# Gate weights in three blocks per half instead of two, and the parameter rows moved from SyncE's load queue to GpSimd's

## The chip, the core and the metric

The kernel runs on one core of a Trainium2 chip. The metric is the device time of one execution in microseconds (us). The core has five engines with a queue each: TensorE (PE, with its weight loads as PEld), VectorE (DVE), ScalarE (ACT), GpSimd (POOL) and SyncE (SP). SP and ACT also issue loads and stores, which 16 DMA engines carry out; in the profile q1 is SP's DMA queue and q10 is ACT's. Each engine runs its instructions in the order of the program and waits on semaphores for the others.

## The reference

What is computed, for one sequence of 2048 tokens with 448 channels:

```python
xn = _layernorm(x)
# A: a diagonal complex state space, 448 states
dt = exp(log_dt); Lam_bar = exp(dt * Lam)
B_bar = ((Lam_bar - 1) / Lam)[:, None] * Bmat
h = Lam_bar[None, :] * h + Bu[:, t, :]          # for every token t
s = 2 * einsum("blp,dp->bld", hseq, Cmat).real + xn * Dskip
# B: a gated unit, 448 -> 1792 -> 448
g = xn @ w_gate; u = xn @ w_up
b = (sigmoid(g) * u) @ w_down
out = x + s * silu(b)
```

## The kernel before

**Tiles and stages.** The tokens are 16 tiles of 128 (x tile t), in four chunks of 512. Each tile is normalised, transposed to channels by tokens (xnT), and multiplied with the gate and up weights: 14 steps a chunk, seven for `g` and seven for `u`. A step makes 256 of the 1792 features of one matrix, 128 with the weights and inputs in partitions 0 to 63 (L688) and 128 with those in 64 to 127 (L689): the 448 channels are seven groups of 64, and each weight matrix lies in one tile, wG or wU, with half of its columns in each half of the partitions. A step writes one of three PSUM buffers (gu). ScalarE takes a `g` step out with a tanh (L702), VectorE a `u` step with the product (L705); only then can the buffer be written again. Between the steps TensorE makes the input of the state space (`b_units`, L736 to L752), which ScalarE copies to bus (L760) and VectorE turns, scans and turns back (`ssm_pair`, L796 to L820; `ssm_stack`, L830 and on), the down projection (L864) and the output of the state space (L889).

**The first chunk** is different. Its gate and up weights are still being loaded. Its four x tiles come in three loads (tile 0 by SP, 1, and 2 with 3, by ACT). `stats` takes mean and variance on VectorE (L421, L422); `chain` takes the root on ScalarE (L430), copies the mean on GpSimd (`meanf`, L431) and inverts the root on VectorE (L432); `norm` (L449) makes xn. TensorE transposes (`pe_transpose`, L481 to L483), and ScalarE (tile 0, L486) or VectorE (L489) copies the result to xnT. `warm_mm` fills TensorE until then. The first three `g` steps are split in halves of tokens: with tiles 0 and 1 as soon as these are there, with tiles 2 and 3 later.

**The loads at the head.** A half of the gate matrix (1792 columns in two halves, 64 partitions each) comes in blocks of steps, which `BLK` lists. Half 0 is loaded by SP, half 1 by ACT, so a block needs a load of each. The three parameter vectors (log_dt, Lambda_im, Lambda_re) are loaded by `load_p` as three rows of one partition each into vrow, a piece of an hF tile. `columns` turns them with five small matmuls (L521, L523) and a copy (L527) into columns pv. GpSimd makes from them, in six small operations from L535 to L544, the step dt, the angle `turn` and the radius `r`. `tables` needs `turn`: ScalarE scales an index row (L556), VectorE reduces the angle (L558, L560), ScalarE takes Abs, Sin and Cos (L563 to L567). `coeffs` (GpSimd) and `c_scale` follow.

After the gate weights SP issues the up weights (two blocks of each half), x tiles 4 to 7, and `dbc`, then the transposed loads of B (L373 by `tload`). x tiles 4 to 7 are the input of chunk 1: `stats` (L421), `chain` on GpSimd (L435, L436) with a reciprocal and a product on VectorE (L438, L439), `norm` on ScalarE (L454), and a skip row on VectorE (L462, `skip_row`).

**What sets the order.** Every operation is handed to a planner (`Plan`), with an engine, an assumed cost, and the keys that it reads (`r`) and writes (`w`). `solve` gives each a due time, backward from a fixed order of TensorE's operations, then plays the program forward with the assumed costs: a free engine takes, of what is ready, what is due first. The instructions are emitted in the order of these planned starts, and each engine then keeps that order. TensorE's order is that of the calls, and VectorE's too while `pl.seq` is set (at the head). So an assumed cost, a rate or a moved call can change the order on the other engines.

**Load slots.** Loads and stores of SP and ACT share eight completion semaphores, taken in turn. The ninth load waits, on its issuing engine and with all that is queued behind it, until the first has landed, and so on. In the program before, SP's second gate block is the ninth and waits for x tile 0, ACT's second gate block is the tenth and waits for the first parameter row, and the first up load, the eleventh, waits for the first gate block. The planner imitates this:

```python
k = o.slot if o.slot < HEAD_DMA else max(HEAD_DMA, len(landed))
if k - 8 in landed:
    o.end = free[e] = max(o.end, landed[k - 8] + o.cost)
```

Loads that GpSimd issues have semaphores of their own and are planned with 6 us from issue to landing.

Of the kernel before, what the change touches and what calls it, by code (L numbers as in the profile page):

```python
# [14 lines left out]
ACT = mybir.ActivationFunctionType  # L15
# [3 lines left out]
D = 448  # L19
# [54 lines left out]
class Plan:  # L74
# [10 lines left out]
    def add(self, eng, cost, fn, r=(), w=(), dma=0, lat=None, chain=False, name="", rate=230e3):  # L85
        o = Op()
        o.idx, o.eng, o.cost, o.fn, o.dma, o.name = len(self.ops), eng, cost, fn, dma, name
        o.lat = LAT.get(eng, 0.0) if lat is None else lat
        o.pre, o.suc, o.rate = {}, [], rate
        o.slot = None  # L90
        if dma and eng != "POOL":
            o.slot, self.n_dma = self.n_dma, self.n_dma + 1
        o.start = o.end = None
        for k in r:
            if k in self.w:
                self._edge(self.w[k], o, True)
        for k in w:
            for q in self.r.get(k, ()):
                self._edge(q, o, False)
            if k in self.w:  # L100
                self._edge(self.w[k], o, True)
        for k in w:
            self.w[k] = o
            self.r[k] = []
        for k in r:
            if k not in w:
                self.r.setdefault(k, []).append(o)
        if chain or eng == "PE" or (eng == "DVE" and self.seq):
            key = ("chain", eng)
            if key in self.last_of:  # L110
                self._edge(self.last_of[key], o, None)
            self.last_of[key] = o
        self.ops.append(o)
        return o
# [131 lines left out]
def kernel(  # L246
# [24 lines left out]
    def sbt(name, shape, dt=BF16):  # L271
        return sb.tile([P] + list(shape), dt, name=name)

    def flat(t, *dims):
        if len(dims) == 1:
            return t
        names = "abcd"[:len(dims)]
        kw = {n: v for n, v in zip(names[1:], dims[1:])}
        return t.rearrange("p (" + " ".join(names) + ") -> p " + " ".join(names), **kw)
# [41 lines left out]
    vrow = hF_raw[0][0:3, 0:448]  # L321
# [10 lines left out]
    def C(name, n=4, dt=FP32):  # L332
        if name not in col:
            col[name] = sbt("c_" + name, [n], dt)
        return col[name]
# [13 lines left out]
    def load(eng, key, nbytes, o, i, cost=0.45, r=(), rate=230e3):  # L349
        e = {"SP": Q, "ACT": A, "POOL": G}[eng]  # L350
        add(eng, cost, lambda: e.dma_start(out=o, in_=i), w=[key] if not isinstance(key, list) else key,  # L351
            r=r, dma=nbytes, chain=True, rate=rate)

    def load_x(t0, n, q="SP", r=(), rate=230e3):
        load(q, [("x", t) for t in range(t0, t0 + n)], n * P * D * 2,
             x_all[:, t0:t0 + n, :], x_src[:, t0:t0 + n, :], r=r, rate=rate)

    BLK = {"g": [(0, 3), (3, 7)], "u": [(0, 3), (3, 7)]}

    def load_w(eng, k, half, b, r=(), rate=105e3):  # L360
        m0, m1 = BLK[k][b]
        ps = slice(half * H, half * H + H)
        c0 = half * 896
        load(eng, [("w", k, half, m) for m in range(m0, m1)], H * 7 * (m1 - m0) * P * 2,
             wgt[k][ps, :, m0 * P:m1 * P],
             wsrc[k][:, c0 + m0 * P:c0 + m1 * P].rearrange("(s p) f -> p s f", p=H), cost=0.65, r=r, rate=rate)
# [22 lines left out]
        add(e, 0.7, lambda: None, chain=True)  # L389
    add("ACT", 0.05, lambda: A.preload_act_table_set("sqrt_and_others"), w=["sqrttab"], lat=1.5, chain=True)  # L390

    def load_p(eng, k):
        load(eng, ("vrow", k), D * 2, vrow[k:k + 1, :], (A_log_dt, A_Lambda_im, A_Lambda_re)[k].unsqueeze(0), cost=0.25)
    load_x(0, 1, "SP")
    load_p("SP", 0)
    load_w("SP", "g", 0, 0)
    load_x(1, 1, "ACT")
    load_x(2, 2, "ACT")
    load_w("ACT", "g", 1, 0)
    load_p("SP", 1)  # L400
    load_p("SP", 2)
    load_w("ACT", "g", 1, 1)
    load_w("SP", "g", 0, 1)
    for h in range(2):
        load_w("SP", "u", h, 0, rate=215e3)
    load_x(4, 4, rate=300e3)
# [60 lines left out]
    def next_acc():  # L467
        a = acc_n[0] % 2
        acc_n[0] += 1
        return a  # L470
# [4 lines left out]
    def pe_transpose(t):  # L475
        b, a, js = t % NXN, next_acc(), slice(t * P, t * P + P)
        tp = flat(acc[a][:].bitcast(BF16)[:, 0:7 * P], 7, P)

        def f():
            for s in range(6):  # L480
                T.transpose(tp[:, s, :], xn[b][:, s * H:s * H + P], ident[:, :])  # L481
            T.transpose(tp[0:H, 6, :], xn[b][:, 384:448], ident[:, :])
            T.transpose(tp[H:P, 6, :], xn[b][:, 0:H], ident[:, :])  # L483
        add("PE", 0.46, f, r=[("xn", b), "ident"], w=[("acc", a)])
        if t == 0:
            add("ACT", 0.85, lambda: A.copy(out=xnT[0][:, :, js], in_=tp[:, :, :]),  # L486
                r=[("acc", a)], w=[("xnT", 0, t, "a"), ("xnT", 0, t, "b")])
        else:
            add("DVE", 0.64, lambda: V.tensor_copy(out=xnT[0][:, :, js], in_=tp[:, :, :]),  # L489
                r=[("acc", a)], w=[("xnT", 0, t, "a"), ("xnT", 0, t, "b")])  # L490
# [9 lines left out]
    def xr(c, lo=0, hi=TPC):  # L500
        return [("xnT", c % 3, j, h) for j in range(lo, hi) for h in "ab"]
# [13 lines left out]
    def columns():  # L515
        a = next_acc()
        vps = flat(acc[a][:, 0:12], 4, 3)

        def f():
            for i in range(3):  # L520
                T.matmul(vps[:, i, :], lhsT=vrow[:, i * P:(i + 1) * P], rhs=ident[0:3, 0:3], start=True, stop=True)  # L521
            for h in range(2):
                T.matmul(vps[h * H:h * H + H, 3, :], lhsT=vrow[:, 384:448], rhs=ident[0:3, 0:3], start=True, stop=True)  # L523
        add("PE", 0.4, f, r=["ident"] + [("vrow", k) for k in range(3)], w=[("acc", a)])
        pv = sbt("pv", [3, 4], FP32)
        dt_b = C("dt", 4, BF16)
        add("DVE", 0.1, lambda: V.tensor_copy(out=pv[:].rearrange("p k i -> p i k"), in_=vps[:]), r=[("acc", a)], w=["pv"])  # L527
        dt_b = C("dt", 4, BF16)
        lim, lre = pv[:, 1, :], pv[:, 2, :]
        K.update(lre=lre, lim=lim)  # L530
        eb = expc[:].to_broadcast((P, 4))

        def small(fn, r, w):
            add("POOL", 0.4, fn, r=r, w=w)
        tt = lambda o, x, y, op: (lambda: G.tensor_tensor(out=o, in0=x, in1=y, op=op))  # L535
        theta, arg, turn, r_col = C("theta"), C("arg"), C("turn"), C("r")
        small(tt(dt_b[:], eb, pv[:, 0, :], ALU.pow), ["pv", "expc"], ["dt"])
        small(tt(theta[:], dt_b[:], lim, ALU.mult), ["dt", "pv"], ["theta"])
        small(lambda: G.tensor_single_scalar(out=turn[:], in_=theta[:], scalar=1.0 / TWO_PI, op=ALU.mult),
             ["theta"], ["turn"])  # L540
        small(lambda: G.tensor_single_scalar(out=turn[H:P, 3:4], in_=theta[H:P, 3:4], scalar=-1.0 / TWO_PI,
                                            op=ALU.mult), ["theta", "turn"], ["turn"])
        small(tt(arg[:], dt_b[:], lre, ALU.mult), ["dt", "pv"], ["arg"])
        small(tt(r_col[:], eb, arg[:], ALU.pow), ["arg", "expc"], ["r"])  # L544
# [135 lines left out]
    def gu_mm(c, k, m, a, lo, hi, first):  # L680
        x = xnT[c % 3]
        ts = slice(lo * P, hi * P)
        w_ = wgt[k]
        ms = slice(m * P, m * P + P)

        def f():
            for s in range(7):
                T.matmul(gu[a][:, 0, ts], lhsT=w_[0:H, s, ms], rhs=x[0:H, s, ts], start=(s == 0), stop=(s == 6))  # L688
                T.matmul(gu[a][:, 1, ts], lhsT=w_[H:P, (s + 1) % 7, ms], rhs=x[H:P, s, ts],  # L689
                         start=(s == 0), stop=(s == 6))  # L690
        n = (hi - lo) * P
        return add("PE", 7 * (0.0028 + n / 2400.0) + (2 * SW if first else 0), f,
                   r=xr(c, lo, hi) + [("w", k, 0, m), ("w", k, 1, m)], w=[("gu", a)], name=f"{k}{c}.{m}")
# [234 lines left out]
    warm_mm(2)  # L928
    gu_mm(0, "g", 0, slots0[0], 0, 2, True)
    gu_mm(0, "g", 1, slots0[1], 0, 2, True)  # L930
    columns()
    pe_transpose(2)
    pe_transpose(3)
    silu_table()
    pl.seq = False
    gu_mm(0, "g", 2, slots0[2], 0, 2, True)
    for m in range(3):
        gu_mm(0, "g", m, slots0[m], 2, 4, False)
        gu_evac(0, "g", m, slots0[m])
# [143 lines left out]
```

## Time and profile before

| | us |
|---|---|
| median of 5 runs (lowest, highest) | 189.85 (188.67, 190.17) |
| the profiled execution | 190.17 |
| its span, first to last instruction | 188.3 |
| TensorE busy in the span | 180.3 |
| VectorE busy in the span | 168.6 |
| end of the warm-up matmuls, first gate matmul | 7.23, 8.94 |
| x tiles 4 to 7: issued, first used | 10.23, 17.80 |
| first L556 (tables) | 13.20 |

The page gives, for each engine, the time in which it was busy, its share of the span and the number of instructions, and then the span in 40 slices of 4.7 us, each with a digit for the busy share in tenths. Lines of waits give who waited, for whom, and how long in total, how often, and at longest. Lines of a timeline give start, duration, engine, line, operation, the tiles written and read, and, in brackets, the idle time before and what ended it. A load's issue and its landing are two things: the issuing queue shows the first, the landing follows some microseconds later.

### The profile page before, as it was taken

What the parts mean: (1) busy time and instruction counts of PE and PEld (TensorE: products, weight loads), DVE (VectorE), ACT (ScalarE), POOL (GpSimd) and SP (SyncE); (2) the same over time, 40 slices, a digit from 0 to 9 for tenths busy, and PEclk for the clock granted to TensorE, in tenths of its full rate; (3) what the DMA queues carried; (4) which work ended last, traced back from release to release, by engine and by line L of the source; (5) the groups of instructions that cost most, each with busy time, mean ns of one, the idle gap of its engine ahead of it and who ended that gap; (6) DMA issues with size and microseconds to landing.
All of it is one profiled execution on the core that took longest, in us unless ns stands there. A gap on an engine that the chain in (4) does not pass through costs nothing.

```text
span 188.3 us, 3507 instructions
## 1 busy us (share of the span) xinstructions
PE 180.3 (96%) x1375; PEld 89.2 (47%) x1375; DVE 168.6 (90%) x303; ACT 87.7 (47%) x124; POOL 32.5 (17%) x84
## 2 busy tenths in 40 slices
PE   7699999999999999999999999999999999999990
PEld 2286554474454444444454445444445445455560
DVE  3836799998999999989999998999999999899943
ACT  3529998735879651244547331337246221502110
POOL 3145447000014560000027800000000000000000
PEclk9999999999999999999999999999999999999999
DMA  6999999499400033200000343000000100000220
GB/s 164 234 208 249 163 135 222 98 248 146 172 3 0 0 77 73 49 0 3 0 2 0 77 101 70 0 28 0 24 3 0 49 0 28 0 24 28 73 77 24
DMA packets 29239, 13.43 MB, mean 71 GB/s; under 512 B 19619, under 2 KB 29222, under 8 KB 29222
## 3 DMA queue, kind: packets, MB, share of 16 engines
q1 hardware_dynamic: 27878, 12.05, 30.7%
q10 hardware_dynamic: 1344, 1.15, 2.6%
q8 instruction: 11, 0.18, 0.4%
q14 instruction: 6, 0.05, 0.1%
HBM read 6.77 MB, written 1.84 MB: 46 GB/s over the span
## 4 chain that ended last, share of the span: by engine, by line
PE 74%; DVE 10%; DMA 6%; SPq 6%; issue 1%; ACT 1%; DVEq 0%
PE gu L688 31%; PE acc L864 17%; PE acc L889 11%; PE gu L749 7%; PE gu L864 6%; DVE hF L705 5%; DMA wG<-in_B_w_gate_dram 4%; SPq L373 3%; SPq L351 3%; DMA bT<-in_A_B_re_dram 2%; DVE xd L462 1%; PE gu L752 1%; PE gu L736 1%; PE gu L889 1%; DVE z L799 1%
## 5 line engine op out<-in xcount | busy, mean ns | idle before, releaser
L688 PE MATMUL gu<-xnT,wG 64*128 64x512 bf16 (+1 forms) x224 | 46.5, 350 | 1.7 <-DMA wG<-in_B_w_gate_dram 1.7
L689 PE MATMUL gu<-xnT,wG 64*128 64x512 bf16 (+1 forms) x224 | 46.4, 350 | 0.0
L688 PE MATMUL gu<-xnT,wU 64*128 64x512 bf16 (+1 forms) x203 | 46.2, 369 | 0.2 <-ACT sig L702 0.2
L689 PE MATMUL gu<-xnT,wU 64*128 64x512 bf16 (+1 forms) x203 | 46.2, 369 | 0.0
L702 ACT ACTIVATE sig<-gu 128x1024 f32<-128x1024 f32 x21 | 21.4, 1022 | 33.3 <-PE gu L689 33.3
L864 PE MATMUL acc<-wd,hF 128*128 128x448 bf16 x168 | 33.8, 353 | 0.0
L864 PEld LDWEIGHTS <-hF 128*128 128x128 bf16 x224 | 21.7, 98 | 20.9 <-issue 1.3
L688 PEld LDWEIGHTS <-wG 64*128 64x128 bf16 x224 | 20.4, 94 | 22.6 <-issue 2.2
L688 PEld LDWEIGHTS <-wU 64*128 64x128 bf16 x203 | 18.8, 94 | 22.1 <-issue 1.3
L705 DVE SCALAR_TENSOR_TENSOR hF<-sig,gu 128x1024 bf16<-128x1024 f32 x21 | 25.5, 1214 | 2.0 <-PE gu L689 1.8
L803 DVE TENSOR_TENSOR_SCAN wv<-c_r,st,z 128x512 bf16<-128x512 f32 x18 | 23.0, 1276 | 0.0
L889 PE MATMUL acc<-cT,hT 128*128 128x448 bf16 x105 | 22.0, 353 | 0.0
L689 PEld LDWEIGHTS <-wG 64*128 64x128 bf16 x224 | 20.3, 94 | 0.4
L689 PEld LDWEIGHTS <-wU 64*128 64x128 bf16 x203 | 18.7, 94 | 0.5 <-issue 0.5
L749 PE MATMUL gu<-xnT,bT 128*128 128x512 bf16 x72 | 16.9, 380 | 0.0
L760 ACT CAST bus<-gu 128x1024 bf16<-128x1024 f32 x12 | 12.1, 1010 | 9.1 <-PE gu L749 8.3
L889 PEld LDWEIGHTS <-hT 128*128 128x128 bf16 x119 | 11.5, 98 | 10.1 <-issue 0.4
L870 ACT ACTIVATE g_t<-acc 128x448 bf16<-128x448 f32 x12 | 6.5, 538 | 18.0 <-PE acc L864 18.0
L435 POOL TENSOR_SCALAR veb<-mv 128x2 bf16<-128x2 bf16 (+1 forms) x5 | 3.8, 754 | 54.3 <-DVE mv L422 54.2
L421 DVE BATCH_NORM_STATS2 bst<-x_all 128x6 f32<-128x448 bf16 x16 | 9.4, 612 | 3.1 <-DMA x_all<-in_A_x_dram 3.1
L864 PE MATMUL gu<-wd,hF 128*128 128x448 bf16 x56 | 11.1, 352 | 0.0
L454 ACT ACTIVATE xn<-x_all,nmr,rsd 128x448 bf16<-128x448 bf16 x12 | 8.4, 765 | 5.5 <-POOL nmr L444 5.4
(132 smaller groups left out, 243.3 us busy)
## 6 DMA issues: line engine op xcount, KB each, us to landing
out_dram<-o_t SPq DMA_DIRECT2D x15, 112.0 KB, 1.7
wd<-in_B_w_down_dram SPq DMA_DIRECT2D x2, 784.0 KB, 5.0
x_all<-in_A_x_dram SPq DMA_DIRECT2D x3, 448.0 KB, 4.9
wU<-in_B_w_up_dram SPq DMA_DIRECT2D x2, 448.0 KB, 8.9
wU<-in_B_w_up_dram SPq DMA_DIRECT2D x2, 336.0 KB, 6.0
wG<-in_B_w_gate_dram ACTq DMA_DIRECT2D x1, 448.0 KB
wG<-in_B_w_gate_dram SPq DMA_DIRECT2D x1, 448.0 KB, 9.7
xnT<-xn SPq DMA_TRANSPOSE x24, 2.4
```

The lines of the kernel that those rows point to most:

```text
L421: add("DVE", 0.6, lambda: V.bn_stats(out=bst[b][:], in_=x_all[:, t, :]), r=[("x", t)], w=[("bst", b)])
L454: add("ACT", 0.65, lambda: A.activation(xn[b][:, 0:448], x_all[:, t, :], ACT.Identity, bias=nmr[:, t, :], scale=rsd[:, t, :]), r=[("x", t) ...
L688: T.matmul(gu[a][:, 0, ts], lhsT=w_[0:H, s, ms], rhs=x[0:H, s, ts], start=(s == 0), stop=(s == 6))
L689: T.matmul(gu[a][:, 1, ts], lhsT=w_[H:P, (s + 1) % 7, ms], rhs=x[H:P, s, ts], start=(s == 0), stop=(s == 6))
L702: add("ACT", act(1024), lambda: A.activation(th, gu[a][:], ACT.Tanh, scale=0.5), r=[("gu", a)], w=[tk])
L705: add("DVE", dve1(1024), lambda: V.scalar_tensor_tensor(out=ho, in0=th, scalar=1.0, in1=gu[a][:], op0=ALU.add, op1=ALU.mult), r=[("gu", a) ...
L749: T.matmul(gu[a][:, i, :], lhsT=bT[:, kt, i, pt * P:pt * P + P], rhs=x[:, 2 * kt, :], start=False, stop=(kt == 2))
L760: add("ACT", act(1024), lambda u=u, a=a: A.copy(out=bus[u][:], in_=gu[a][:]), r=[("gu", a)], w=[("bus", u)])
L803: dve(1.194, lambda k=k: V.tensor_tensor_scan(out=wv[:, k, :], data0=rb, data1=z[:, k, :], initial=(st[pt][:, k, :] if c else 0.0), op0=AL ...
L864: T.matmul(d, lhsT=hF[c % 2][:, m, h, js], rhs=wd[:, ft, :], start=(ft == 0), stop=(ft == FT - 1))
L870: add("ACT", act(448), lambda: A.activation(g_t[g][:], d, ACT.Silu, scale=0.5), r=[key, "silutab"], w=[("gt", g)])
L889: T.matmul(y, lhsT=hT[c % 2][:, hm, js], rhs=cT[:, cm, c0:c1], start=(i == 0), stop=(i == 6))
```

## The change

The gate weights come in blocks of two, two and three steps instead of three and four. The parameter rows are issued by GpSimd, after the index row (`iota`, the key `("wv", 0)`), and no longer lie between the gate blocks in SP's queue. So nine loads of SP and ACT stand ahead of the up weights (three of x, six of gate weights) instead of ten (three of x, four of gate weights, three rows). The planner is given a lower rate for the first blocks, and a cost of 0.75 for issuing a row. `columns` is called after the third `g` step's first half instead of before the transposes of tiles 2 and 3.

```diff
-    BLK = {"g": [(0, 3), (3, 7)], "u": [(0, 3), (3, 7)]}
+    BLK = {"g": [(0, 2), (2, 4), (4, 7)], "u": [(0, 3), (3, 7)]}
...
-    def load_p(eng, k):
-        load(eng, ("vrow", k), D * 2, vrow[k:k + 1, :], (A_log_dt, A_Lambda_im, A_Lambda_re)[k].unsqueeze(0), cost=0.25)
+    def load_p(eng, k, r=()):
+        load(eng, ("vrow", k), D * 2, vrow[k:k + 1, :], (A_log_dt, A_Lambda_im, A_Lambda_re)[k].unsqueeze(0), cost=0.75, r=r)
     load_x(0, 1, "SP")
-    load_p("SP", 0)
-    load_w("SP", "g", 0, 0)
+    load_w("SP", "g", 0, 0, rate=90e3)
+    load_w("SP", "g", 0, 1)
     load_x(1, 1, "ACT")
     load_x(2, 2, "ACT")
-    load_w("ACT", "g", 1, 0)
-    load_p("SP", 1)
-    load_p("SP", 2)
+    load_w("ACT", "g", 1, 0, rate=90e3)
+    load_w("SP", "g", 0, 2)
     load_w("ACT", "g", 1, 1)
-    load_w("SP", "g", 0, 1)
+    load_w("ACT", "g", 1, 2)
+    load_p("POOL", 0, [("wv", 0)])
+    load_p("POOL", 1)
+    load_p("POOL", 2)
     for h in range(2):
         load_w("SP", "u", h, 0, rate=215e3)
...
     gu_mm(0, "g", 1, slots0[1], 0, 2, True)
-    columns()
     pe_transpose(2)
     pe_transpose(3)
     silu_table()
     pl.seq = False
     gu_mm(0, "g", 2, slots0[2], 0, 2, True)
+    columns()
     for m in range(3):
```

## The prediction

> **What bounds the kernel now.** I read the page's slices first, then the waits by engine, then the timelines of TensorE and VectorE.
>
> ```profile
> span 188.3 us, 3507 instructions
> ...
> PE 180.3 (96%) x1375; PEld 89.2 (47%) x1375; DVE 168.6 (90%) x303; ACT 87.7 (47%) x124; POOL 32.5 (17%) x84
> ...
> PE   7699999999999999999999999999999999999990
> ...
> DVE  3836799998999999989999998999999999899943
> ...
> DMA  6999999499400033200000343000000100000220
> ```
>
> TensorE is full from the third slice (4.7 us each) to the end; VectorE nearly so from the sixth; the DMA engines are full in the first 45 us only. So TensorE can lose only at the start, and a later start of VectorE's full stretch is hard to make good. The waits (engine, line, what it waited for: us in total, times, longest):
>
> ```profile
> PE gu L688 <- DMA wG<-in_B_w_gate_dram: 1.7, 1, 1.7
> ...
> SPq L351 <- DMA wG<-in_B_w_gate_dram: 5.1, 1, 5.1
> ```
>
> The first is the target of the change: the first gate matmul starts at 8.94 when gate weights land, 1.71 us after the warm-up matmuls end. The second is the load slot of the first up-weight load. But neither says what a start earlier is worth. For that I follow VectorE (start, duration, idle before):
>
> ```profile
> 17.80 0.63 DVE L421 BATCH_NORM_STATS2 bst<-x_all 128x6 f32<-128x448 bf16 x1 [1.05 <-DMA x_all<-in_A_x_dram]
> ...
> 22.60 0.18 DVE L438 RECIPROCAL rsd<-sdb 128x4 f32<-128x4 bf16 x1 [0.93 <-POOL sdb L436]
> ...
> 29.46 1.22 DVE L705 SCALAR_TENSOR_TENSOR hF<-hF,gu 128x1024 bf16<-128x1024 bf16 x1
> 30.59 0.69 DVE L462 TENSOR_TENSOR xd<-xn,dbc 128x448 bf16<-128x448 bf16 x2
> ...
> 41.63 1.21 DVE L705 SCALAR_TENSOR_TENSOR hF<-sig,gu 128x1024 bf16<-128x1024 f32 x1
> 42.76 0.68 DVE L817 TENSOR_TENSOR ta<-wv,cosT 128x1024 bf16<-128x1024 bf16 x1
> ```
>
> It waits for x tiles 4 to 7 until 17.80, takes their statistics, waits for GpSimd's power until 22.60, and from there has practically no gap until 43. TensorE meets it twice:
>
> ```profile
> 30.82 0.38 PE L736 MATMUL gu<-xnT,bT 64*128 64x512 bf16 x1
> ...
> 42.42 0.38 PE L736 MATMUL gu<-xnT,bT 64*128 64x512 bf16 x1
> 42.90 0.37 PE L736 MATMUL gu<-xnT,bT 64*128 64x512 bf16 x1
> ```
>
> The matmul at 30.82 needs the bank that the L705 of 29.46 has freed by 30.68: 0.14 us to spare. The one at 42.90 should follow 0.22 after 42.42 and comes 0.48 after it, when the L705 of 41.63 is over (42.84): TensorE is held 0.26 us by VectorE. So **VectorE's stretch from 22.60, which hangs on the landing of x tiles 4 to 7, is the second bound**, and a lead of TensorE over it above some 0.14 us is lost at 30.82.
>
> **What the skill says.** "DMA: Bandwidth & Descriptors", section "Issuing engines are not separate DMA queues": loads from SP, ACT and GpSimd share the same 16 engines, and more issuers save issue time only. The trace agrees: from 5 to 7 us ACT's queue q10 takes 96.3% of the engines and SP's q1 7.7%. The same page, "Why a DMA increments its semaphore by 16 and not by 1": data are there when the last of 16 engines has reported. The trace's landing records show that: fourteen engines finished SP's first gate block by 5.91, the last at 8.90; for ACT's block fifteen by 7.57 and the last at 9.12. One slow engine sets the start. "SBUF — State Buffer", section "SBUF: two separate sides": GpSimd cannot write its DMA descriptors while VectorE runs a two-port operation. VectorE is idle from 1.11 to 3.20, when these loads would be issued, so I expect no such stall; no run here shows one.
>
> **Part 1, the first block, 3 steps to 2.** The slow engine is through with x tiles 2 and 3 at 4.57 and had 28 packets of each first block to move: 56 packets of 768 B in 4.55 us, 81 ns each. Now it has 56 packets of 512 B. In proportion to bytes they take 3.0 us, at an unchanged cost per packet 4.55. The page's "Why small descriptors are slow" gives bytes/32 + 3 cycles (it states the penalty for 256 B): 19 against 27, so 0.70, an estimate of 3.2 us. I take that: landing at 7.8, bounds 7.6 to 9.1. TensorE cannot start before the second tile's copy (6.74 + 0.62) anyway, about 7.45. Lead at the start: 8.94 - 7.8 = 1.1 us, bounds 0 to 1.5.
>
> **Part 2, the later blocks.** The third gate step needs block 1 after two half steps (1.77 us) and two transposes (1.23), at 10.8. The slow engine has 56 more packets of 512 B by then: 7.8 + 3.2 = 11.0, a stall of 0.2, covered by the lead. Block 2 is needed at about 15.7 and comes before 15.
>
> **Part 3, all gate bytes, and x tiles 4 to 7 behind them.** These tiles lie in q1 behind all gate weights and two up blocks; bytes are unchanged, packets are not. One engine had 56 packets of 768 B (mean 55.9 ns in the trace) and 56 of 1024 B (77.7), 7.5 us; it gets 112 of 512 B and 56 of 768 B. With 0.70 x 55.9 = 39 ns that is 7.5 us again. But the first packets of a block on many engines are slow in this trace (0.2 to 0.4 us at 3.3 to 3.7 and at 10.5 to 11.1, against 0.056), and there is one more block on each queue. I add 0.2 for each: **x tiles 4 to 7 land 0.4 us later.** Bounds: a straight line through the two packet times gives 34 ns and, without a slow start, -0.5; an unchanged 55.9 ns per packet gives +1.9.
>
> **Part 4, slots and parameter rows.** Ten loads for eight slots become nine; the last still waits for x tile 0, landed at 3.17, when it would be issued anyway: nothing. The first up load need not be issued before 8.9: half the gate bytes are still ahead of it in q1, so nothing either. SP loses three issues (0.31, 0.45, 0.30). On GpSimd three issues come between its last setup instruction (ends 2.01) and the means of tiles 0 and 1 (L431 at 4.11 and 4.83), on which the normalised tiles, the transposes and the first matmul wait. The trace shows no load by GpSimd: from SP's 0.3 to about 1 us each, the first-byte time in the page's "Specifications". They end between 2.9 and 5.0. At the worst the first mean ends at 5.2 against the 4.82 of the reciprocal that the normalisation waits for as well, and the start can't be before 7.85: covered, just. The rows are needed at 11.6, so their landing is hidden.
>
> **Part 5, columns() behind the third step.** TensorE's 0.28 us move, nothing is added. But the tables hang on it: the first L556 came at 13.20, 2.06 us after the columns (ends 11.14). Now the columns end at 7.8 + 4.06 = 11.9, the turn is there at 13.9, and by then ScalarE, which was free until 13.20, has from 12.8 three evictions (2.83 us) that are due earlier. So the first two L556 move from 13.2 to after 15.6, and with them two pairs L558 + L560 on VectorE, 2 x 1.14 = 2.3 us, which lay in idle time before 17.80. They go behind the statistics: 0.93 fits into the wait before 22.60; 1.4 lands in the full stretch. Cover there: eight skip-row products L462 (about 0.3 us each), due much later, which the planner can move to the next idle stretch (0.96 us at 46.2). I take 0 net, bounds -0.3 to +1.3.
>
> **Sum.** Lead of TensorE 1.1, used only up to where VectorE lets it: the 0.26 at 42.90 can go, since another order of L830 and L705 frees the bank earlier: -0.26. x tiles later: +0.4. Tables: 0. Together +0.15. After that TensorE is full to the end, so it goes through. The profiled execution took 190.17 (span 188.3 and 1.9 around it), the slowest of five; on the median of 189.85 I get 190.0, taken as **190.1**. A measurement of this kernel can tell about 0.5% (0.95 us) from no change.
>
> **Rivals.**
> *Forecast, no change (0.40):* the lead is lost against VectorE. For it: 0.14 us to spare at 30.82.
> *Faster (0.27):* the slow engine is slow because of what is removed, the queueing of the single-partition rows between gate blocks (q1 moves only 0.03 MB from 5 to 7). Then x tiles 4 to 7 land with the other fifteen engines, 16.7 instead of 17.8, VectorE's stretch moves by 1.1 and TensorE's lead lasts: 189.85 - 1.1 = 188.7. Against it: GpSimd's rows share the same engines, and the slow engine has single packets of 0.4 to 0.7 us that are no rows.
> *Slower (0.33):* 512 B packets on the engines' path of x tiles 4 to 7. At 50 ns each, one engine has 112 x 50 + 56 x 55.9 = 8.7 us of gate instead of 7.5: 1.2 later, with the 0.4 of block starts 1.6, less 0.26 of slack: 191.2. It decides from 44 ns up: there the tiles are 1.0 us late, and any half microsecond of tables in the full stretch makes it more than 0.95.
> *The change does not do what it says (within the first):* if block 0 lands near 9.1, no lead, and only Part 3 is left: 190.2.
>
> Range: the bounds of Part 3 and the two outer cases give 188.6 to 191.5; 0.2 is left outside.
>
> **What would show it.** Right: L688 first at 7.5 to 8.2; TensorE held by L705 before 31, in sum about the lead; first L421 of tile 4 at about 18.2, L438 at about 23.0. Part 3 wrong: that L421 before 17.3 (faster) or after 19 (slower). Part 5 wrong: VectorE idle over 1 us between 23 and 43, or the first L556 before 14.5. Part 4 wrong: the first L431 ends after 5.3. The prediction fails if TensorE starts earlier and is nowhere held afterwards.

## The result, and the profile after

The changed kernel takes **189.19 us** in the median (188.37 to 190.55, 43 runs), beside 189.99 for the kernel before (188.67 to 191.71, 80 runs). The ratio is **0.996, 95% interval 0.9948 to 0.9971**: 0.8 us faster. The forecast was +0.25 us, so the kernel moved the other way. It moved by less than the 0.5% that the prediction took as the limit of what can be told, and yet clear of zero. Executions more than 1.5% above the fastest of their kernel are left out of medians and ratios; the profiled one of this first measurement (191.28 us) is among them, so the lines below are of a second measurement of the same kernel, called E1 (189.66 us). The functions stand two lines lower than before: L688 is now L690, L705 is L707, L421 is L423, L436 is L438, L438 is L440, L736 is L738.

The page and its slices:

```profile
span 187.8 us, 3509 instructions
...
PE 180.0 (96%) x1368; PEld 88.4 (47%) x1375; DVE 168.0 (89%) x303; ACT 88.1 (47%) x124; POOL 34.1 (18%) x87
...
PE   7999999999999999999999999999999999999990
...
DVE  3741999999999999999999998999999999899943
...
DMA  5999999499400045200000441000000100000220
```

The span is 0.5 us shorter. VectorE (3836799998 before) now has its hole in the fourth slice (14.1 to 18.8 us), where the tables stood that are now late, and is full from the fifth on. TensorE's start, the warm-up matmuls first:

```profile
1.18 4.88 PE L417 MATMUL gu<-hF 128*128 128x512 bf16 x11 [1.18 <-DVE hF L376]
5.85 0.85 PE L483 MATMUL acc<-ident,xn 128*128 128x128 bf16 x6
...
8.37 0.27 PE L690 MATMUL gu<-xnT,wG 64*128 64x256 bf16 x1 [0.28 <-DVE xnT L491]
```

The wait for gate weights is gone. But the eleven warm-up matmuls take 4.88 us here and not 4.05 as before, and the first six transposes 0.85 instead of 0.51: the gate starts only 0.57 us earlier than it did (8.94), limited by xnT. VectorE:

```profile
17.84 0.63 DVE L423 BATCH_NORM_STATS2 bst<-x_all 128x6 f32<-128x448 bf16 x1 [5.15 <-DMA x_all<-in_A_x_dram]
...
22.37 0.18 DVE L440 RECIPROCAL rsd<-sdb 128x4 f32<-128x4 bf16 x1 [0.33 <-POOL sdb L438]
...
32.69 0.69 DVE L464 TENSOR_TENSOR xd<-xn,dbc 128x448 bf16<-128x448 bf16 x2
...
41.41 1.21 DVE L707 SCALAR_TENSOR_TENSOR hF<-sig,gu 128x1024 bf16<-128x1024 f32 x1
```

x tiles 4 to 7 come at the same time as before (17.80), and yet the reciprocal comes 0.23 us earlier (22.60), and so does the L707 at 41.41 (41.63). The first skip row after it is put off to 32.69; it stood at 24.83. TensorE is held by VectorE at the two places that the prediction named:

```profile
30.42 0.37 PE L738 MATMUL gu<-xnT,bT 64*128 64x512 bf16 x1 [0.23 <-DVE hF L707]
...
42.68 0.37 PE L738 MATMUL gu<-xnT,bT 64*128 64x512 bf16 x1 [0.28 <-DVE hF L707]
```

The second of these waits was there before (0.26 us) and is there in every profile of this order, also in E7 and E11 (0.29 us), whose x tiles come 3 us earlier. So only the first, at 30.42, goes with late x tiles.

Two more lines of the kernel before show what is missing after:

```profile
21.20 1.37 POOL L436 TENSOR_TENSOR sdb<-veb,halfc 128x4 bf16<-128x4 bf16 x1
```

```profile
109.14 0.37 PE L688 MATMUL gu<-xnT,wU 64*128 64x512 bf16 x1 [0.20 <-ACT sig L702]
```

The same power of GpSimd (the root of the variances of tiles 4 to 7, on which the reciprocal waits) is 1.10 us long after, and no idle time of TensorE is left near 109 us. Both come from the order of the instructions and not from a load: E6 below has the loads of before, and shows both.

### The profile page after: what moved, and what is told of

The parts are those of the page before. It is cut to its first block, busy times and chain, and to the rows that moved or that the text cites. A ratio compares the mean times of both kernels' runs of the same rounds, so it can differ in the third digit from the quotient of the medians.

```text
span 189.4 us, 3516 instructions
## 1 busy us (share of the span) xinstructions
PE 180.6 (95%) x1375; PEld 88.1 (47%) x1375; DVE 168.0 (89%) x303; ACT 88.3 (47%) x124; POOL 34.5 (18%) x87
## 4 chain that ended last, share of the span: by engine, by line
PE 80%; DMA 9%; DVE 7%; issue 1%; POOL 1%; SPq 1%; DVEq 0%
PE gu L690 34%; PE acc L866 17%; PE acc L891 11%; PE gu L751 9%; DMA x_all<-in_A_x_dram 6%; PE gu L866 6%; DVE hF L707 4%; DMA wG<-in_B_w_gate_dram 3%; PE gu L754 1%; PE gu L738 1%; DVE bst L423 1%; SPq L351 1%; PE gu L891 1%; POOL sdb L438 1%; PE gu L691 1%
## 5 line engine op out<-in xcount | busy, mean ns | idle before, releaser
L690 PE MATMUL gu<-xnT,wG 64*128 64x512 bf16 (+1 forms) x224 | 46.6, 350 | 0.3 <-DVE xnT L491 0.3
L690 PE MATMUL gu<-xnT,wU 64*128 64x512 bf16 (+1 forms) x203 | 46.4, 369 | 0.5 <-DVE hF L707 0.5
L690 PEld LDWEIGHTS <-wG 64*128 64x128 bf16 x224 | 20.4, 94 | 21.8 <-issue 3.0
L690 PEld LDWEIGHTS <-wU 64*128 64x128 bf16 x203 | 18.8, 94 | 22.5 <-issue 1.3
L707 DVE SCALAR_TENSOR_TENSOR hF<-sig,gu 128x1024 bf16<-128x1024 f32 x21 | 25.5, 1216 | 1.4 <-PE gu L691 1.3
L751 PE MATMUL gu<-xnT,bT 128*128 128x512 bf16 x72 | 16.9, 380 | 0.0
L423 DVE BATCH_NORM_STATS2 bst<-x_all 128x6 f32<-128x448 bf16 x16 | 9.4, 613 | 8.5 <-DMA x_all<-in_A_x_dram 8.5
L437 POOL TENSOR_SCALAR veb<-mv 128x2 bf16<-128x2 bf16 (+1 forms) x5 | 3.0, 601 | 46.8 <-DVE mv L424 46.6
```

The costliest lines, as they stand in the source:

```text
L423: add("DVE", 0.6, lambda: V.bn_stats(out=bst[b][:], in_=x_all[:, t, :]), r=[("x", t)], w=[("bst", b)])
L707: add("DVE", dve1(1024), lambda: V.scalar_tensor_tensor(out=ho, in0=th, scalar=1.0, in1=gu[a][:], op0=ALU.add, op1=ALU.mult), r=[("gu", a) ...
L751: T.matmul(gu[a][:, i, :], lhsT=bT[:, kt, i, pt * P:pt * P + P], rhs=x[:, 2 * kt, :], start=False, stop=(kt == 2))
```

## The experiments

All ratios are to the kernel before, run beside on the same chip (its medians: 189.96 beside E1 to E4, 189.97 beside E5 to E8, 189.72 beside E9 to E12). The ratio is estimated on its own and is not the quotient of the two medians; the two differ by up to 0.12% (E8).

| run | median us | ratio | 95% interval |
|---|---|---|---|
| E1 after, again | 189.10 | 0.9951 | 0.9929 to 0.9972 |
| E2 order of before, loads of after | 189.68 | 0.9994 | 0.9976 to 1.0012 |
| E3 order of after, loads of before | 189.40 | 0.9975 | 0.9960 to 0.9990 |
| E4 after, later start | 189.74 | 0.9996 | 0.9979 to 1.0013 |
| E5 after, columns early | 190.70 | 1.0036 | 1.0015 to 1.0057 |
| E6 before, columns late | 189.48 | 0.9979 | 0.9961 to 0.9996 |
| E7 after, x tiles ahead | 189.11 | 0.9952 | 0.9931 to 0.9972 |
| E8 before, x tiles ahead | 189.67 | 0.9972 | 0.9955 to 0.9989 |
| E9 after, nine warm-ups | 189.16 | 0.9962 | 0.9946 to 0.9978 |
| E10 before, nine warm-ups | 190.19 | 1.0025 | 1.0008 to 1.0042 |
| E11 after, x ahead, nine warm-ups | 188.52 | 0.9933 | 0.9907 to 0.9959 |
| E12 before, rows by GpSimd, columns late | 189.67 | 0.9996 | 0.9976 to 1.0016 |

**E1 to E3: order or loads?** E1 is the changed kernel. 

> The changed kernel itself, once more beside the other three, to read it undisturbed. All theories: about 189.2. They differ in the profile. Theory V (x tiles 4 to 7 come earlier): the first L423 of tile 4 at or before 17.5, where the kernel before had L421 at 17.80, and L440 before 22.4. Theory O (another order of VectorE's work): L423 at 17.8 or later, and yet the last L707 of the stretch or the end of it earlier against L440 than before. Theory P (the start alone): L690 first at about 7.4 and no more than 0.3 us of waiting for L707.

E2 and E3 exchange the two halves of the change: the planner sees one kernel's list and so makes its order, and the loads issued are the other's.

```diff
 # E2, in before.py
...
+    p0_.fn, p1_.fn, p2_.fn = (lambda k=k: row(G, k) for k in range(3))
+    g00_.fn = lambda: (g_block(Q, 0, 0, 2), g_block(Q, 0, 2, 4))
+    g10_.fn = lambda: (g_block(A, 1, 0, 2), g_block(A, 1, 2, 4))
+    g01_.fn = lambda: g_block(Q, 0, 4, 7)
+    g11_.fn = lambda: g_block(A, 1, 4, 7)
 # E3, in after.py
...
+    p0_.fn = p1_.fn = p2_.fn = g12_.fn = lambda: None
+    g00_.fn = lambda: (row(Q, 0), g_block(Q, 0, 0, 3))
+    g01_.fn = lambda: (row(Q, 1), row(Q, 2))
+    g02_.fn = lambda: g_block(Q, 0, 3, 7)
+    g10_.fn = lambda: g_block(A, 1, 0, 3)
+    g11_.fn = lambda: g_block(A, 1, 3, 7)
```

E2: 

> The kernel before with its own order of every engine's work, but the loads of the changed kernel: three gate blocks, parameter rows by GpSimd. The parameter columns stay at their early place. Theory V (the loads carry it): 189.2, as the changed kernel. Theory O (the order of the compute engines carries it): 190.0, as before. Theory P (TensorE's start is passed through): some 188.9 to 189.3.

E3: 

> The changed kernel with its order of every engine's work, but the loads of the kernel before: two gate blocks, parameter rows on SyncE between them. The columns come behind the third step. Theory V: 190.0, as before. Theory O: 189.2, as the changed kernel. Theory P: 190.0 to 190.3, with a first L690 at about 8.9.

Measured: the new loads with the old order (E2) gain 0.06%, nothing that can be told. The new order with the old loads (E3) gains 0.25%, about half of the change: between theory O's 189.2 and the 190.0 of the others. With the new loads the order is worth more: E1 and E2 issue the same loads, differ by 0.58 us in the median, and their intervals do not overlap. Those of E1 and E3, which share the order, do, so what the loads add to it is not shown by this pair. E1's x tiles come at 17.84, against theory V (earlier x tiles); its first gate matmul at 8.37 and 0.5 us of waiting for L707 speak against theory P. In E2 TensorE waits for the third row, since the columns are still early (L536 there is L521 before):

```profile
10.14 0.21 PE L536 MATMUL acc<-ident,hF 3*128 3x3 bf16 x3 [0.50 <-DMA hF<-in_A_Lambda_re_dram]
```

The third row landed at 10.01 here. In E5, also with early columns, it landed at 9.62 and TensorE did not wait. So the late columns make room for rows loaded by GpSimd, and they bring an order of their own.

**E4: is the start passed through?**

```diff
-    def warm_mm(n):
+    def warm_mm(n, extra=0):
...
-            for _ in range(n):
+            for _ in range(n + extra):
...
-    warm_mm(2)
+    warm_mm(2, 5)
```

> The changed kernel with five more warm-up matmuls ahead of the first gate step, which keep TensorE from that step for about 1.1 us; loads and all orders unchanged. Theories V and O (TensorE's lead at the start is lost against VectorE anyway): 189.2 to 189.5, and the wait for L707 gets shorter by about what the start is later. Theory P: 190.2, all of the 1.1 us is seen at the end.

Measured 189.74: 0.6 us over E1 by the medians, of some 1.1 added, and the intervals do not overlap. So theories V and O, by which the lead is lost anyway, do not hold, and neither does theory P, by which all of it counts. In the profiled execution the late start cost nothing: it came at 8.25 only, later than all but E1's (8.37) among the profiles with these loads, and the span is 187.5 against E1's 187.8, since the x tiles came earlier (17.52). So which of the two chains ends last may differ from one execution to the next.

**E5 and E6: the place of the columns alone.** E5 moves `columns()` in the changed kernel back to its early place, E6 moves it in the kernel before to the late one; the loads stay.

E5: 

> The changed kernel with columns() back at its early place, ahead of the third gate step; the loads stay as changed. The order written out for VectorE, ScalarE and GpSimd goes back almost to that of the kernel before with it. Theory C (the late columns bring the better order: 0.27 us at GpSimd's power for x tiles 4 to 7, 0.20 us at the TensorE stall at 109 us): 189.6 to 189.8, the power at about 1.37 us again, and TensorE idle by 0.2 us near 109 again. Theory L (the loads alone, by the earlier start): 189.2, as the changed kernel.

E6: 

> The kernel before with columns() behind the third gate step and nothing else; loads unchanged. Theory C: 189.4 to 189.6, power at about 1.1 to 1.2 us, no stall near 109 us, with TensorE's first gate step still at about 8.6 to 8.9. Theory L: 190.0, as before.

E6 met theory C: 0.21% faster by one moved call, with the power at 1.11 us (20.84 to 21.95) and no stall near 109. E5 went further than either theory: 0.36% slower than before. Its timeline of VectorE and TensorE says why:

```profile
16.91 0.63 DVE L423 BATCH_NORM_STATS2 bst<-x_all 128x6 f32<-128x448 bf16 x1 [1.20 <-DMA x_all<-in_A_x_dram]
...
22.82 1.18 DVE L464 TENSOR_TENSOR xd<-xn,dbc 128x448 bf16<-128x448 bf16 x3
23.91 1.21 DVE L707 SCALAR_TENSOR_TENSOR hF<-hF,gu 128x1024 bf16<-128x1024 bf16 x1
```

```profile
30.93 0.37 PE L738 MATMUL gu<-xnT,bT 64*128 64x512 bf16 x1 [0.64 <-DVE hF L707]
```

Planning with the new loads, the planner put three skip rows, 1.18 us that nobody waits for, ahead of the first L707. It starts 7.00 us after the x tiles (5.90 before: 23.70 - 17.80; 5.43 in E1: 23.27 - 17.84), and TensorE pays 0.64 us at 30.93. The x tiles came earlier here (16.91) than in any other profile in which their load keeps its place, and it did not make up for that.

**E7 and E8: take the second bound away.** SyncE issues x tiles 4 to 7 ahead of the first two up-weight blocks, in the changed kernel (E7) and in the one before (E8); compute orders unchanged.

```diff
     load_x(4, 4, rate=300e3)
+    u0_, u1_, x4_ = pl.ops[-3:]
+    u0_.fn, u1_.fn, x4_.fn = x4_.fn, u0_.fn, u1_.fn
```

E7: 

> The changed kernel with the load of x tiles 4 to 7 given to SyncE ahead of the first two up-weight blocks instead of behind them; order of the compute engines unchanged. If two bounds run side by side (TensorE: first gate step + 179.2 us; VectorE: first statistics of tile 4 + 170.0 us; 1.9 us around the larger), the second falls by 2 to 3 us and TensorE's early start is all that is left: 188.5 to 188.9, the first statistics of tile 4 at about 15, no wait for L707 before 32. If the landing of these tiles does not bound the changed kernel in most executions: 189.2.

E8: 

> The kernel before with the same exchange of loads, order of the compute engines unchanged. With two bounds side by side the late first gate step (8.6 to 8.9) bounds it now as it did before: 189.7 to 190.0, less than 0.3 us gained. If VectorE's stretch alone bounds the kernel before: 188.5 to 189.0.

E7's tiles come 3.44 us earlier than E1's, and the time is E1's. It did not reach the 188.5 to 188.9 expected. The chain had moved to TensorE's start (the lines of E7 stand two lower again):

```profile
1.18 4.87 PE L419 MATMUL gu<-hF 128*128 128x512 bf16 x11 [1.18 <-DVE hF L376]
...
8.10 0.27 PE L692 MATMUL gu<-xnT,wG 64*128 64x256 bf16 x1 [0.28 <-DVE xnT L493]
```

```profile
14.40 0.63 DVE L425 BATCH_NORM_STATS2 bst<-x_all 128x6 f32<-128x448 bf16 x1 [2.00 <-DMA x_all<-in_A_x_dram]
```

From 8.10 to the end of the span (187.2) are 179.1 us, which is what E6 shows too (187.5 - 8.41 = 179.09). In the kernel before the same edit gains 0.28% (E8; 0.30 us by the medians, where less than 0.3 was expected). This fits x tiles that bind there in a part of the executions, but does not show it: the profile of E8 is of a quick execution (189.00 us) that started at 7.79, and how the starts of the others lie is not on record.

**E9 to E11: take the first bound away.** Six of the eleven profiles with eleven first warm-up matmuls have them end between 5.9 and 6.1 us, later than the first normalised tile (5.2 to 5.5); in the others they end at 5.0 to 5.5. E9 runs nine of them in the changed kernel (`warm_mm(11, -2)`, with E4's helper), E10 in the one before, E11 in E7's.

E9: 

> The changed kernel with 9 instead of 11 warm-up matmuls at the start; all orders unchanged. In five of the nine profiles so far of this kernel and its variants the eleven took 4.8 to 4.9 us (0.43 us each almost to the end) and ended near 6.05, after the first normalised tile (5.35); in the others the rate doubled at about 4 and they ended by 5.5. Theory W (these warm-up matmuls are what bounds the start of the changed kernel in half of the executions): nine end by 5.2 at the latest, the start moves by up to 0.7 us in those, 0.2 to 0.4 us in the median: 188.7 to 188.9. Rival (the rate only doubles after a certain amount of work): transposes and the first gate step run at the lower rate for longer: 189.1 to 189.6. Rival (VectorE's stretch bounds): 189.1.

E10: 

> The same edit in the kernel before. Theory W: its first gate step waits for the gate weights in most executions, so the length of the warm-up is hidden: 189.8 to 190.0. If the start is not what tells the two kernels apart: the same gain as in the changed kernel.

E11: 

> Both edits in the changed kernel: x tiles 4 to 7 ahead of the up weights, and 9 warm-up matmuls. With two bounds side by side each edit alone can be stopped by the other bound, the two together are not: 188.5 to 188.8. If neither bound is set there: 189.1.

E9 alone gains nothing over E1 (0.9962 against 0.9951). Its profile starts early, and then loses all of it to VectorE, whose x tiles came late in this execution:

```profile
7.42 0.27 PE L690 MATMUL gu<-xnT,wG 64*128 64x256 bf16 x1 [0.27 <-DVE xnT L491]
```

```profile
18.35 0.63 DVE L423 BATCH_NORM_STATS2 bst<-x_all 128x6 f32<-128x448 bf16 x1 [6.62 <-DMA x_all<-in_A_x_dram]
```

The waits of TensorE in it, and then in E11 (L740 and L709 there are L738 and L707):

```profile
PE gu L738 <- DVE hF L707: 1.0, 2, 0.7
...
PE gu L690 <- DVE hF L707: 0.6, 1, 0.6
```

```profile
PE gu L740 <- DVE hF L709: 0.3, 1, 0.3
```

E11, with both edits, starts at 7.58, has its x tiles at 14.55, and a span of 186.7. It is the fastest version: 0.67% under the kernel before. Only six runs were taken, and its interval overlaps with that of the changed kernel (0.9951, or 0.996 in the larger sample). But all six (188.32 to 188.86) lie below the median of E9 (189.16), and below 15 of its 21 runs; E9 ran beside it on the same chip and differs by the place of the x tiles alone. E10 was to stay at 189.8 to 190.0 and came out 0.25% slower. Its profile has x tiles at 18.37, a span that this explains (below), and all twelve transposes at the low rate (0.82 for six); why it is slower in the median stays open.

**E12: rows out of SyncE's queue, but two blocks.**

```diff
-    load_p("SP", 0)
...
-    load_p("SP", 1)
-    load_p("SP", 2)
...
+    load_p("POOL", 0, [("wv", 0)])
+    load_p("POOL", 1)
+    load_p("POOL", 2)
...
-    columns()
     pe_transpose(2)
...
     gu_mm(0, "g", 2, slots0[2], 0, 2, True)
+    columns()
```

> The kernel before with the parameter rows loaded by GpSimd and the columns behind the third step, but still two gate blocks of three and four steps. If the blocks of two steps bring what the loads bring: 189.5, as with the late columns alone. If the rows between the gate blocks in SyncE's queue held the first block back: 189.1 to 189.2, as the changed kernel.

No gain (0.9996), rather less than E6, though the intervals overlap. It does not tell the rows from the blocks, because one more thing changed with the edit. Only seven loads now stand ahead of the up weights, so the first two of these are issued at 2.62 and 3.36 (8.91 and 9.56 before) and run beside the gate blocks. The first gate block landed at 8.47 and 8.88 (SyncE's and ScalarE's half), hardly earlier than before (8.90 and 9.12). Blocks of two without moved rows were not tried.

## Why the prediction was right or wrong

**Two bounds, not one behind the other.** Each profile gives three numbers: first gate matmul (P), first statistics of x tile 4 (V), span. Four constants describe them: the span is the larger of P + 179.1 and V + 170.0 with late columns (the order of after, or one close to it in E6 and E12), and of P + 179.3 and V + 170.5 with the order of before. They are read from E6, E7 and E11 (179.1), E1, E4 and E9 (170.0), E8 and before (179.3), before and E10 (170.5), so only the other rows test them. E2, E3 and E12 come out within 0.2, and so does the first measurement, whose x tiles came later than in any other profile (19.35).

| profile | P | V | by P | by V | span |
|---|---|---|---|---|---|
| before | 8.94 | 17.80 | 188.2 | 188.3 | 188.3 |
| E8 | 7.79 | 15.59 | 187.1 | 186.1 | 187.1 |
| E10 | 8.14 | 18.37 | 187.4 | 188.9 | 188.8 |
| E2 | 7.94 | 17.75 | 187.2 | 188.3 | 188.4 |
| E1 | 8.37 | 17.84 | 187.5 | 187.8 | 187.8 |
| E3 | 8.57 | 17.07 | 187.7 | 187.1 | 187.8 |
| E4 | 8.25 | 17.52 | 187.4 | 187.5 | 187.5 |
| E6 | 8.41 | 17.45 | 187.5 | 187.5 | 187.5 |
| E7 | 8.10 | 14.40 | 187.2 | 184.4 | 187.2 |
| E9 | 7.42 | 18.35 | 186.5 | 188.4 | 188.4 |
| E11 | 7.58 | 14.55 | 186.7 | 184.6 | 186.7 |
| E12 | 8.52 | 17.85 | 187.6 | 187.9 | 188.1 |
| after, first measurement | 7.34 | 19.35 | 186.4 | 189.4 | 189.4 |

E5 alone falls out (188.5 against 187.4), by the 1.1 us that its skip rows put before the first L707 (7.00 against 5.90). In the profile of before the two tie. The late columns lower P's constant by 0.2 and V's by 0.5: the 0.2 of both is the stall near 109 us, and the further 0.27 of V's is the shorter power; both are taken up below.

**The sum: the steps that failed.** VectorE's stretch was rightly found as the second bound. But all three terms of the sum were off. The columns, put at 0, brought -0.4 (E6, below), which is the part of the gain that experiments show (E3 and E6). The x tiles, put at +0.4, came at 17.84 in E1 against 17.80. And the lead of TensorE was written off but for the 0.26 us at 42.90, on the ground that VectorE binds in every execution. Those 0.26 us did not go (0.28 at 42.68 in E1), and the rest of the lead was not always lost: E4 shows 0.6 of 1.1 us at the end, and in E7 3.4 us of x tiles are worth nothing. V scatters from 16.9 to 19.4 in the profiles in which the load of the x tiles keeps its place, and P from 7.8 to 8.9 with the old loads. A tie in one profile should have been read as "either, from run to run", not as "the lead is lost".

**Part 5, columns: priced 0, with -0.3 to +1.3; E6 measured -0.4** (0.21%, interval 0.04 to 0.39%). The tables did move (first L558 at 16.10, said: after 15.6), and the planner did put the skip rows off, as was argued. So the mechanism that was priced is there, and it is not what counted. Missed were two gains of order. First the stall of 0.20 near 109 us, which is there in before, E2, E5, E8 and E10, and in no profile with late columns. Second GpSimd's power. "SBUF — State Buffer" of the Trainium skill, section "SBUF: two separate sides", says that VectorE and GpSimd share a pair of ports, that certain VectorE operations (two-port modes, or two inputs in SBUF) take it for the whole instruction, and that the other then waits. The traces agree in the timing. Before (first line) and E1 (the other two), where L560 is the L558 of before:

```profile
20.99 0.69 DVE L560 SCALAR_TENSOR_TENSOR hT<-hT,hT 128x513 f32<-128x513 f32 x1
```

```profile
20.38 1.06 DVE L560 TENSOR_SCALAR hT<-hT 128x513 f32<-128x513 f32 x3
...
21.23 1.10 POOL L438 TENSOR_TENSOR sdb<-veb,halfc 128x4 bf16<-128x4 bf16 x1
```

In all thirteen profiles in which a VectorE instruction was running when this power began, the power ended 0.89 to 0.90 us after that instruction's end: before at 22.57, after the two-input L560 that ends at 21.68; in E1 at 22.33, after the last of the three L560, which end at 21.44. With 0.21 us of the instruction left it took 1.10 us (E1), with 0.33 it took 1.23 (E3), with 0.36 1.25 (E11), with 0.48 1.37 (before), and with VectorE idle 1.06 (E7). The later powers of the same traces, of half the size, are a control for the kind of instruction. With some 0.42 us left of a VectorE instruction they took 0.73 us beside the statistics L423, which read one tile of SBUF, and 1.01 us beside L820, a product of two tiles in SBUF, each in all fourteen profiles; beside an idle VectorE they took 0.73 too. E1:

```profile
54.98 0.68 DVE L820 TENSOR_TENSOR tb<-wv,spm 128x1024 bf16<-128x1024 bf16 x1
...
55.23 1.01 POOL L438 TENSOR_TENSOR sdb<-veb,halfc 128x2 bf16<-128x2 bf16 x1
...
97.22 0.60 DVE L423 BATCH_NORM_STATS2 bst<-x_all 128x6 f32<-128x448 bf16 x1
...
97.40 0.73 POOL L438 TENSOR_TENSOR sdb<-veb,halfc 128x2 bf16<-128x2 bf16 x1
```

Two things are not as the page has it, or not shown. The next two-input VectorE instruction, which in E1 began at 21.36 with the power under way, took its usual 0.68 us, where by the page one of the two should have waited. And E1's L560 has one input: that it runs in a two-port mode no run shows. The prediction named the shared port for the row loads only, and did not look at who runs beside L436.

**Part 1, the start: 7.8 foreseen, 8.37 in E1 (7.34 to 8.10 in the other profiles with these loads, E4 with its longer warm-up apart).** The landing was better than foreseen: both halves of the first block were there by 7.09 in E1 and by 6.83 to 7.82 in the six other variants with these loads, against 8.05 to 9.12 with blocks of three. Only in the first measurement ScalarE's half came late, at 8.42. But TensorE was not ready. What the trace of before could not show is the scatter of the warm-up: 3.85 to 4.88 us for the same eleven matmuls in eleven profiles, hidden before by the wait for weights. The place to look was "TensorE: Matmul & The Clock Gate" of the skill, in "Part 1: The HAM clock gate": the first matmuls run at half rate until an activity window that does not start with the kernel has passed, so their number varies. It gives 426.7 and 215.7 ns from start to start for 512 columns; the traces show 0.43 us at first and 0.22 later. So in six of the eleven profiles the floor lay later than the "about 7.45" of the prediction.

**Part 3, x tiles: +0.4 foreseen, +0.04 in E1.** Packets of 512 B took 32.5 ns each in E1 (both queues), not the 39 estimated from the page; the 768 B ones 56.2. The bound of 34 ns by the straight line was nearer. Over the profiles with this load in its place V is 16.9 to 19.4 with the new loads and 17.1 to 18.4 with the others, so a shift of 0.4 could not be told from the scatter. In the changed kernel earlier tiles alone are worth nothing (E7).

**Part 4: right.** Three issues by GpSimd took 0.76, 0.51 and 0.50 us (1.82 to 3.59), the first mean came at 4.14 (4.11 before). The rows landed by 9.6: in time for the late columns, and for early ones only at times (E2, E5).

**The rivals.** The faster one had the sign, but the x tiles did not come at 16.7. Its reason, the rows, is not settled by E12, and the landings speak for a part of it: with the rows in SyncE's queue the last of the 16 engines finished SyncE's first gate block 0.65 to 2.99 us after the fourteenth (five profiles), without them 0.16 to 0.78 (nine profiles; 0.50 in E12). The slower one needed 50 ns a packet; there were 32.5. Together: of the 0.8 us the order brings 0.4 (E6; 0.5 in E3). The rest, 0.4, is a difference. That it is the earlier start, about half a microsecond in P where V lets it, fits E4 and E11, but no run shows it apart from the order and clear of the noise.

## What to carry to other kernels

When a profile shows two chains that end within some tenths of each other, take neither as hidden: price the change against both, with their scatter from run to run, and test with an edit that eases both (E11), because an edit of one alone can be stopped by the other (E7, E9). Where a planner writes the order, a moved call is a change of order everywhere: E6 gained 0.4 us by it, and in E5 the call moved back left the changed kernel 0.7 us slower than the kernel before, with hardly a cost of its own. And once a start no longer waits for data, look at what was hidden by that wait, here the warm-up.

## What was not expected of the hardware

The same eleven warm-up matmuls take 3.85 to 4.88 us, 0.43 us each at first and 0.22 later, with the change of rate at another moment from one execution to the next. A GpSimd power on 128x4 takes 1.06 us beside an idle VectorE and 1.10 to 1.37 beside a busy one, depending on when the VectorE instruction ends that was running at its start; on 128x2 it takes 1.01 beside a product of two tiles in SBUF, and 0.73 beside statistics of one tile, as beside an idle VectorE. Packets of 512 B take 0.58 of the time of 768 B ones (32.5 against 56.2 ns), less than the proportion of bytes (0.67).
